# Nystrom attention and a top-1 expert layer on one core: q and k of three batches turned on TensorE, the pseudo-inverse on eight tiles and in pairs, output in blocks of 32 rows, a refitted planner

## Chip, cores, metric

One of the cores of a Trainium2 chip runs one program. The metric is the device time of one execution in microseconds; lower is better. Input and output lie in device memory.

## What is computed

Eight batches of eight heads, 576 positions, head size 64. Nystrom attention with 32 landmarks (each the mean of 18 neighbouring positions), then an expert layer over the 4608 rows, in which each row goes to the expert with the greatest logit.

```python
q_lm = q.reshape(B, H, m, S // m, D).mean(axis=3)      # m = 32; k_lm the same from k
A, Bm, C = sm(q, k_lm), sm(q_lm, k_lm), sm(q_lm, k)    # softmax of scaled products
Z = Bm.T / (norm1(Bm) * norminf(Bm) + 1e-06)
for _ in range(6):
    Z = 2 * Z - Z @ Bm @ Z
x = (A @ Z @ C @ v)                                    # -> (4608, 512)
e = argmax(x @ w_gate)
out = softmax(x @ w_gate)[e] * sigmoid(x @ w_output_gate)[e] * (relu(x @ w1[e]) @ w2[e])
```

Attention is in f32, the expert layer in bf16. The kernel takes for each batch its most frequent expert as the main one. Rows of other experts are done by a loop at the end that reads a count of them and is skipped when it is zero.

## The kernel before

**Attention of a batch** (`batch`, from line 388) goes in two halves of four heads, 32 partitions a head and landmark. SyncE brings k, q and v (lines 403 and 406) into three buffers each. VectorE turns k and q in blocks of 32 x 32 (line 415). The landmark sums are five additions, which the planner gives to GpSimd or VectorE (434 to 438), and a turn of the sums (442). TensorE makes the scores of k and q against the landmarks from 32 x 32 tiles, two passes over the head size (459, 461). The scores of k go through a maximum (466), an exponential on ScalarE (470, 471), six turns on TensorE (480), an evacuation (482) and the product with v (491). Those of q are turned, normalised over the landmarks and turned back on VectorE, GpSimd and ScalarE (508 to 529).

**The pseudo-inverse** (533 to 611) of a batch: the scores of landmarks (542), a softmax, column sums, and seven iterations. An iteration is 16 small matmuls (587: X'X and X'Y of four heads, first one half and then the other, on the same four 32 x 32 tiles of the array) and a step on VectorE, 2X minus the product in PSUM (597, 602, 605). Batch 0 takes its halves as steps of their own.

**Routing** (613 to 731): the result is turned, multiplied by the gates and by the attention weights (627, 639); VectorE finds the expert of each row and the batch's main one in some twenty small instructions (656 to 709). Then x is formed (720) and written as bf16.

**The expert layer** (733 to 787): GpSimd reads the main expert and brings its w1 and w2 in halves, with a cast to bf16, by eight DMAs (335, 338, 342), into one of two buffers (even and odd batches); a load whose expert is already in the buffer is skipped. For the up product 8 x 2 blocks of four matmuls of 128 x 288 (759) are evacuated with a relu on ScalarE (365). For the down product five tiles of rows, four of 128 and one of 64, are eight matmuls of 512 columns each (774), scaled (781 or 783) into one of four y buffers and written out by one DMA a tile (786), whose access pattern is 4 (or 2) positions x 32 landmarks x 512.

**The order of the work** isn't written out. Each operation is given to `Plan` (72 to 234) with its engines and costs in ns, its reads and writes, a priority (`PR` by batch for attention, `FR` for the expert layer, lines 269 and 270) and a mode (the tile shape on TensorE). `run` plays a list schedule with these costs, chooses engine and buffer for each, and emits the instructions in the order of their planned starts. On the chip each engine then takes its instructions strictly in that order. `CAPA` and `CAPF` limit the PSUM banks in use by attention and by the expert layer.

Of the kernel before, what the change touches and what calls it, by code (L numbers as in the profile page):

```python
# [22 lines left out]
F32 = mybir.dt.float32  # L23
# [43 lines left out]
class Op:  # L67
    __slots__ = ("engs", "fn", "deps", "new", "vals", "prio", "lag", "end", "eng", "nd", "succ", "load", "seq",
# [3 lines left out]
class Plan:  # L72
# [3 lines left out]
    LAT = 90.0  # L76
    PE_LAG = 150.0
# [4 lines left out]
    FETCH = 3800.0  # L82

# [5 lines left out]
    def op(self, engs, fn, r=(), w=(), hold=(), prio=0.0, lag=0.0, load=0.0, mode=None, after=(), bias=0.0, shy=(), recs=0):  # L89
# [8 lines left out]
        o.deps = set(after)  # L98
        o.new = []
# [19 lines left out]
        for v in o.vals:  # L119
            if v in o.new:  # L120
                v.first = o
            if v.tag is not None:
                o.deps.add(v.first)
            v.users.add(o)
        o.deps.discard(o)
        self.ops.append(o)
        return o

    def run(self):
        free = {}  # L130
        for o in self.ops:
            o.nd = len(o.deps)
            o.succ = []
        for o in self.ops:
            for d in o.deps:
                d.succ.append(o)
# [6 lines left out]
        dma = 0.0  # L143
# [4 lines left out]
        while ready:  # L148
            cands = []
            for o in ready:  # L150
# [19 lines left out]
                for e, c in o.engs.items():  # L170
                    st = max(free.get(e, 0.0), slot_t)
                    for d in o.deps:
                        st = max(st, d.end + (self.LAT if d.eng != e else 0.0))
                    if e == "PE" and o.mode != mode:
                        st = max(st, free.get(e, 0.0) + self.SWITCH)
                    cands.append((st, st + c, o, e))
# [5 lines left out]
            for st, en, o, e in cands:  # L182
                if o not in best_per or en + o.shy.get(e, 0.0) < best_per[o][1] + o.shy.get(best_per[o][2], 0.0):
# [5 lines left out]
                    key=lambda p: (p.prio, p.seq))  # L189
            st, en, e = best_per[o]  # L190
# [15 lines left out]
            free[e] = en  # L206
            busy[e] = busy.get(e, 0.0) + en - st
            if o.load:
                dma = max(dma, en) + o.load
                o.end = dma + o.lag  # L210
            else:
                o.end = en + o.lag + (self.PE_LAG if e == "PE" else 0.0)
# [25 lines left out]
def kernel(  # L238
# [28 lines left out]
    SHY = 1100.0  # L267
    SHYE = 400.0
    PR = [0.0, 1.0, 2.0, 3.0, 4.0, 5.0, 6.0, 7.0]
    FR = [3.5, 4.5, 5.5, 5.25, 7.5, 8.5, 9.5, 10.5]  # L270
    PESUM = 0
    SPLIT = (0,)
    CAPA = 2
    CAPF = 2
    LASTF = 5
    LOAD = 2050.0
    WLOAD = 5000.0
# [14 lines left out]
    e8 = pool.tile([128, E], F32, name="e8")  # L292
    e0 = pool.tile([128, E], F32, name="e0")
    pad = pool.tile([128, E], F32, name="pad")
    wgs = pool.tile([128, HH, 2 * E], F32, name="wgs")
# [14 lines left out]
    t_lm = tag("lm", 4, [128, 2, 2, m])  # L310
    t_EC = tag("EC", 1, [128, 2, U2])
    t_ECT = tag("ECT", 1, [PT, 6, 128])
    t_At = tag("At", 2, [128, g, m])
    t_AT = tag("AT", 4, [128, UP])
    t_XW = tag("XW", 2, [128, 2, m + D])
    t_X = tag("X", 4, [128, 2, m + D])
    t_sm = tag("sm", 8, [128, 64])
    t_co = tag("co", B, [128, NT])
    t_ZT = tag("ZT", 2, [128, 128])
    t_G = tag("G", 2, [128, 2, m])  # L320
    t_lg = tag("lg", 2, [128, NT, m])
    t_rt = tag("rt", 2, [128, 8, NT, E])
# [9 lines left out]
    def ask_w1(dst, e, part, **new):  # L332
        f_ = slice(part * F // 2, (part + 1) * F // 2)
        w = moe_w1[bass.ds(e, 1)]
        nc.gpsimd.dma_start(out=dst[:, :2, f_], in_=w.rearrange("e (c p) f -> p (e c) f", p=128)[:, :2, f_], **new)  # L335
        src = w.rearrange("e (c a p) f -> a p (e c) f", a=2, p=D)
        for a in range(2):
            nc.gpsimd.dma_start(out=dst[a * D:(a + 1) * D, 2:, f_], in_=src[1 - a, :, 2:, f_], **new)

    def ask_w2(dst, e, part, **new):  # L340
        c_ = slice(part * FCH // 2, (part + 1) * FCH // 2)
        nc.gpsimd.dma_start(out=dst[:, c_], in_=moe_w2[bass.ds(e, 1)].rearrange("e (c p) d -> p (e c) d", p=128)[:, c_], **new)

    with tc.manual_schedule():
# [5 lines left out]
        nc.vector.tensor_copy(e0, ei)  # L350
        ri = pool.tile([128, B, NT], I32, name="ri")
        for h in range(HH):
            nc.gpsimd.iota(ri[h * m:(h + 1) * m], pattern=[[S, B], [HH, NT]], base=h, channel_multiplier=g)
        nc.vector.tensor_copy(rows, ri)
        nc.vector.tensor_scalar(out=e8, in0=e0, scalar1=8.0, scalar2=None, op0=ADD)
        for t in t_AT.tiles:
            nc.gpsimd.memset(t[:, S:], 0.0)
        for t in t_G.tiles:
            nc.gpsimd.memset(t, 0.0)

# [15 lines left out]
        def evac(n):  # L376
            return {"ACT": 140 + 0.95 * n, "DVE": 90 + 1.1 * n}
# [4 lines left out]
        def bring_gates(e):  # L382
            for hf in range(2):
                for i, w in enumerate((moe_w_gate, moe_w_output_gate)):
                    nc.sync.dma_start(out=wgs[hf * D:(hf + 1) * D, :, i * E:(i + 1) * E],
                                      in_=w[hf * HH * D:(hf + 1) * HH * D].rearrange("(h d) e -> d h e", d=D))

        def batch(b):
            pr = PR[b]
            lms, ATs, sms, ZVp = [], [], [], []  # L390
            XW = Val(t_XW)
            P.op({"": 0}, lambda e: None, w=[XW["home"]], prio=pr)
            for hf in range(2):
# [14 lines left out]
                if b == 0 and hf == 1:  # L408
                    P.op({"SP": 2500}, bring_gates, w=[gates[0]], prio=pr, lag=2500)
                    P.op({"POOL": 400}, lambda e: nc.gpsimd.tensor_scalar(  # L410
                        out=wgs[:, :, E:], in0=wgs[:, :, E:], scalar1=-1.0, scalar2=None, op0=MUL),
                        w=[gates[0]], prio=pr + .5)
                Ts = {"q": Val(t_T["q"]), "k": Val(t_T["k"])}
                for x in "kq":
                    P.op({"DVE": 1370}, lambda e, T=Ts[x], n=ns[x], x=x: nc.vector.transpose(  # L415
                        out=T.t.rearrange("p j (t r) -> p t j r", r=m) if x == "q" else
                        T.t.rearrange("p j (t w r) -> p w t j r", t=6, w=3),
                        in_=n.t.rearrange("p t (j c) -> p t j c", j=2) if x == "q" else
                        n.t.rearrange("p (w t) (j c) -> p w t j c", j=2, w=3)),
                        r=[ns[x][0]], w=[Ts[x][0]], prio=pr + .01)  # L420
                s9 = Val(t_s9) if b >= PESUM else Val(p_M, "attn", CAPA)
                for i, x in ((1, "k"), (0, "q")):
                    if b < PESUM:
                        def sums_pe(e, n=ns[x], s9=s9, i=i):
                            for t in range(g):
                                nc.tensor.matmul(s9.t[:, i * D:(i + 1) * D], lhsT=I128, rhs=n.t[:, t, :],
                                                 start=(t == 0), stop=(t == g - 1))
                        P.op({"PE": 2050}, sums_pe, recs=72, r=[ns[x][0]], w=[s9[i]], mode=(128, 128), prio=pr + .005)
                        continue
                    s3 = Val(t_s3)  # L430

                    def sums(e, n=ns[x], s9=s9, s3=s3, i=i):
                        eng = nc.gpsimd if e == "POOL" else nc.vector
                        eng.tensor_tensor(s3.t, n.t[:, :9], n.t[:, 9:], op=ADD)  # L434
                        eng.tensor_tensor(s3.t[:, :4], s3.t[:, :4], s3.t[:, 4:8], op=ADD)
                        eng.tensor_tensor(s3.t[:, :2], s3.t[:, :2], s3.t[:, 2:4], op=ADD)
                        eng.tensor_tensor(s3.t[:, 0], s3.t[:, 0], s3.t[:, 1], op=ADD)
                        eng.tensor_tensor(s9.t[:, i], s3.t[:, 0], s3.t[:, 8], op=ADD)
                    P.op({"POOL": 3200, "DVE": 1750}, sums, r=[ns[x][0]], w=[s9[i], s3[0]], prio=pr + .005, shy={"DVE": SHY})
                lm = Val(t_lm)  # L440
                lms.append(lm)
                P.op({"DVE": 270}, lambda e, lm=lm, s9=s9: nc.vector.transpose(  # L442
                    out=lm.t.rearrange("p x j r -> p (x j r)"),
                    in_=s9.t[:, :128] if b < PESUM else s9.t.rearrange("p x d -> p (x d)")),
                    r=[s9[0], s9[1]], w=[lm[0]], prio=pr + .02)
# [5 lines left out]
                sms.append(st)  # L451

                def scores(e, pC=pC, pA=pA, lm=lm, Ts=Ts):
                    for n in range(2):
                        for j in range(2):
                            for h in range(HH):
                                r_ = slice(h * m, (h + 1) * m)
                                o = (h + 2) % HH
                                nc.tensor.matmul(pC.t[o * m:(o + 1) * m, n, :U2], lhsT=lm.t[r_, 0, j, :],  # L459
                                                 rhs=Ts["k"].t[r_, j, n * U2:(n + 1) * U2], start=(j == 0), stop=(j == 1))  # L460
                                nc.tensor.matmul(pA.t[r_, n, :U2], lhsT=lm.t[r_, 1, j, :],  # L461
                                                 rhs=Ts["q"].t[r_, j, n * U2:(n + 1) * U2], start=(j == 0), stop=(j == 1))
                P.op({"PE": 1950}, scores, recs=128, r=[lm[0], Ts["k"][0], Ts["q"][0]], w=[pC[0], pA[0]], hold=[EC, At, st],
                     mode=(32, 32), prio=pr + .03)

                P.op({"DVE": 760}, lambda e, pC=pC, st=st: nc.vector.tensor_reduce(  # L466
# [6 lines left out]
                P.op({"ACT": 1150}, c_exp, r=[pC[0], st[0]], w=[EC[0], st[1]], prio=pr + .03)  # L473
# [3 lines left out]
                def ec_turn(e, pE=pE, EC=EC):  # L477
                    f = EC.t.rearrange("p a c -> p (a c)").rearrange("p (t c) -> p t c", t=6)
                    for c in range(6):
                        nc.tensor.transpose(pE.t[:PT, c // 3, (c % 3) * 128:(c % 3 + 1) * 128], in_=f[:, c], identity=I128)  # L480
# [391 lines left out]
```

## Time and profile before

| what | value |
|---|---|
| three runs | 336.76, 338.63, 343.56 us; median 338.63 |
| the profiled execution | 341.74 us, span 340.1 us |
| TensorE | busy 265.4 us, 78% of the span, mean granted clock 0.913 |
| VectorE | busy 199.5 us, 59% |
| ScalarE, GpSimd | busy 146.3 and 137.7 us |
| DMA | 49.02 MB in 28294 packets, mean 144 GB/s |

A row of a group reads: line, engine, operation, output<-input with shapes, count | busy us in all, mean ns of one | idle us of the engine just before them, and what ended it. A row of the timeline reads: start us, length us, engine, line, operation, count. Lines are those of the kernel before. Durations of matmuls overlap, since they are pipelined.

### The profile page before, as it was taken

The numbers are of one execution on the slowest core, as the hardware profiler recorded it, in microseconds if no ns is written. First come the engines' busy times: TensorE is split into PE (matmuls) and PEld (weight loads), VectorE is DVE, ScalarE is ACT, GpSimd is POOL, SyncE is SP. The second block draws the span as 40 slices with busy tenths as digits, with TensorE's granted clock in tenths as the row PEclk, the third lists the DMA queues.
The fourth block names the chain that finished last, engine by engine and source line by source line (L and its number), as shares of the span: only waits on it lengthen the run. The fifth ranks groups of instructions, "written<-read, shape, count | busy, mean of one in ns | idle before, by whom it ended". The sixth has DMA issues, their size and how long they took to land. (4 is left out here: it accounts for less than half of the span.)

```text
span 340.1 us, 10916 instructions
## 1 busy us (share of the span) xinstructions
PE 265.4 (78%) x4525; PEld 169.9 (50%) x4537; DVE 199.5 (59%) x542; ACT 146.3 (43%) x356; POOL 137.7 (40%) x225
## 2 busy tenths in 40 slices
PE   0466755896998799599899997399999975996950
PEld 0134543464745477457557755276667433654520
DVE  4698978797897896689816936459441430500000
ACT  1033233245535555156465743157365332743420
POOL 3659899569766973752001213232020060150000
PEclk9956969699999799899999999789999995999795
DMA  7999747559958977476212315817021159196221
GB/s 279 255 328 255 212 143 202 125 139 206 191 162 235 201 237 189 108 220 232 94 53 77 83 39 160 139 17 114 2 64 63 40 123 209 33 168 130 91 84 62
DMA packets 28294, 49.02 MB, mean 144 GB/s; under 512 B 3152, under 2 KB 19536, under 8 KB 28240
## 3 DMA queue, kind: packets, MB, share of 16 engines
q1 hardware_dynamic: 17360, 37.79, 35.9%
q0 software_dynamic: 10880, 10.49, 20.1%
q8 instruction: 37, 0.61, 0.7%
q14 instruction: 17, 0.14, 0.1%
HBM read 61.90 MB, written 9.44 MB: 210 GB/s over the span
## 5 line engine op out<-in xcount | busy, mean ns | idle before, releaser
L759 PE MATMUL M<-xT_all,w 128*128 128x288 bf16 x512 | 75.2, 298 | 19.3 <-DMA w<-in_moe_w_dram 11.9
L774 PE MATMUL M<-w,hT 128*128 128x512 bf16 (+1 forms) x309 | 73.6, 381 | 0.6
L759 PEld LDWEIGHTS <-w 128*128 128x128 bf16 x512 | 50.3, 102 | 38.5 <-issue 12.6
L365 ACT ACTIVATE hT<-M 128x288 bf16<-128x288 f32 x128 | 50.4, 410 | 31.6 <-PE M L759 27.4
L459 PE MATMUL S<-Tk,lm 32*32 32x288 f32 x512 | 43.6, 467 | 11.4 <-DVE lm L442 11.4
L774 PEld LDWEIGHTS <-hT 128*128 128x128 bf16 (+1 forms) x320 | 30.8, 101 | 33.5 <-issue 1.1
L461 PE MATMUL S<-Tq,lm 32*32 32x288 f32 x512 | 41.1, 465 | 0.0
L781 ACT ACTIVATE y<-M,co 128x512 f32<-128x512 f32 (+1 forms) x38 | 25.8, 685 | 34.1 <-PE M L774 24.7
L335 POOL DMA_DIRECT2D w<-in_moe_w_dram x16 | 7.8, 489 | 74.1 <-DVE X L602 35.4
L459 PEld LDWEIGHTS S<-Tk,lm 32*32 32x32 f32 x512 | 25.2, 119 | 18.3 <-DVE lm L442 11.1
L587 PE MATMUL M<-X 32*32 32x96 f32 x768 | 26.8, 252 | 9.2 <-DVE X L602 6.8
L516 POOL TENSOR_TENSOR At<-At,sm 128x576 f32<-128x576 f32 x16 | 18.6, 1161 | 30.6 <-DVE sm L511 23.4
L602 DVE SCALAR_TENSOR_TENSOR X<-X,M 128x192 f32<-128x192 f32 (+1 forms) x45 | 13.9, 315 | 27.6 <-PE M L587 27.6
L587 PEld LDWEIGHTS M<-X 32*32 32x32 f32 x768 | 17.4, 107 | 23.1 <-DVE X L602 8.4
L525 POOL TENSOR_TENSOR At<-At,sm 128x576 f32<-128x576 f32 x16 | 18.7, 1166 | 24.9 <-DVE sm L523 15.8
L470 ACT ACTIVATE sm<-sm 128x1 f32<-128x1 f32 x16 | 3.2, 203 | 51.7 <-DVE sm L466 51.7
L367 ACT CAST xT_all<-S 128x576 bf16<-128x576 f32 x31 | 18.6, 640 | 13.7 <-PE S L720 13.7
L434 POOL TENSOR_TENSOR s<-nk 128x576 f32<-128x576 f32 x13 | 18.3, 1407 | 14.9 <-DMA nk<-in_k_dram 8.0
L529 DVE STREAM_TRANSPOSE AT<-At 128x576 f32<-128x576 f32 x16 | 12.3, 769 | 17.7 <-POOL At L525 10.3
L480 PE MATMUL S<-I,EC 128*96 128x128 f32 x96 | 16.1, 313 | 7.9 <-ACT EC L471 5.4
L415 DVE STREAM_TRANSPOSE Tk<-nk 128x1152 f32<-128x1152 f32 x16 | 21.7, 1358 | 0.1
L415 DVE STREAM_TRANSPOSE Tq<-nq 128x1152 f32<-128x1152 f32 x16 | 21.5, 1346 | 0.0
(111 smaller groups left out, 406.2 us busy)
## 6 DMA issues: line engine op xcount, KB each, us to landing
nk<-in_k_dram SPq DMA_DIRECT2D x16, 576.0 KB
nq<-in_q_dram SPq DMA_DIRECT2D x16, 576.0 KB
nv<-in_v_dram SPq DMA_DIRECT2D x48, 192.0 KB
w<-in_moe_w_dram POOLq DMA_DIRECT2D x16, 512.0 KB
out_dram<-y SPq DMA_DIRECT2D x32, 256.0 KB
w<-in_moe_w_dram POOLq DMA_DIRECT2D x16, 256.0 KB
w<-in_moe_w_dram POOLq DMA_DIRECT2D x32, 128.0 KB
out_dram<-y SPq DMA_DIRECT2D x8, 128.0 KB
```

The source lines that it names most:

```text
L365: nc.scalar.activation(out=dst(), in_=src(), func=RELU)
L367: nc.scalar.copy(dst(), src())
L415: P.op({"DVE": 1370}, lambda e, T=Ts[x], n=ns[x], x=x: nc.vector.transpose(out=T.t.rearrange("p j (t r) -> p t j r", r=m) if x == "q" else ...
L434: eng.tensor_tensor(s3.t, n.t[:, :9], n.t[:, 9:], op=ADD)
L459: nc.tensor.matmul(pC.t[o * m:(o + 1) * m, n, :U2], lhsT=lm.t[r_, 0, j, :], rhs=Ts["k"].t[r_, j, n * U2:(n + 1) * U2], start=(j == 0), sto ...
L461: nc.tensor.matmul(pA.t[r_, n, :U2], lhsT=lm.t[r_, 1, j, :], rhs=Ts["q"].t[r_, j, n * U2:(n + 1) * U2], start=(j == 0), stop=(j == 1))
L516: P.op({"POOL": 1160}, lambda e, At=At, st=st: nc.gpsimd.tensor_tensor(At.t, At.t, b_l(st.t[:, 8:8 + g]), op=SUB), r=[st["ax"]], w=[At[0]] ...
L525: P.op({"POOL": 1160}, lambda e, At=At, st=st: nc.gpsimd.tensor_tensor(At.t, At.t, b_l(st.t[:, 32:32 + g]), op=MUL), r=[st["as"]], w=[At[0 ...
L587: nc.tensor.matmul(pN.t[r_, hf * W:(hf + 1) * W], lhsT=cur.t[r_, hf, :m], rhs=cur.t[r_, hf, :])
L759: nc.tensor.matmul(ph.t[:, :NH], lhsT=w1.t[:, dc, fc * 128:(fc + 1) * 128], rhs=xT.t[:, dc, n * NH:(n + 1) * NH], start=(dc == 0), stop=(d ...
L774: nc.tensor.matmul(py.t[:tk, :], lhsT=hTs[fc].t[:, i * 128:i * 128 + tk], rhs=w2.t[:, fc, :], start=(fc == 0), stop=(fc == FCH - 1))
L781: nc.scalar.activation(out=y.t[:tk], in_=py.t[:tk, :], func=COPY, scale=com.t[:tk, i:i + 1])
```

## The change

1. **q and k of batches 0 to 2** (`PET = 3`) are turned on TensorE: 18 turns of 128 x 128 a half into PSUM, and evacuations of 512 and 128 columns by ScalarE or VectorE. The sums are turned by four matmuls. The scores of these batches then contract over 64 rows in one pass, 16 matmuls a half instead of 32.
2. **The pseudo-inverse** keeps its two halves on eight tiles of the array (half 1 shifted by two column groups, in a second bank) and accumulates in PSUM; factors of two and the sign are in the scaling. A step is a plain scaled copy, in three pieces, on ScalarE or VectorE. Batches 4 and 5, and 6 and 7, are solved together.
3. **Output**: a DMA writes 32 rows (SP: four a tile; the last two tiles of the last batch go half from SP and half from ScalarE's queue). The tile of 64 rows is made as two halves of 256 columns on two column groups, and scaled as one 128 x 256 tile.
4. **Smaller ones**: position order by even and odd; w1 in two DMAs of 64 partitions, and in whole loads for batches 2 to 5 (`WHALF`); the gates as one 128-row product; fewer small routing instructions; a row sum on VectorE in one instruction; a relu may go to VectorE; the count of strays formed once at the end.
5. **The planner**: new costs, latencies and priorities, three banks each for attention and expert layer, a rule that lets an engine wait for a more urgent operation.

```diff
-    LAT = 90.0
-    PE_LAG = 150.0
+    LAT = 50.0
+    SAME = 34.0
+    LAG = 95.0
+    PE_LAG = 185.0
+    DRAIN = {(32, 64): 178.0, (128, 32): 140.0, (64, 32): 125.0, (32, 32): 125.0, (128, 64): 130.0}
...
+            better = [p for p in best_per if best_per[p][2] == e and p.prio < o.prio - self.MARGIN
+                      and best_per[p][0] < best_per[o][1]]
...
-    FR = [3.5, 4.5, 5.5, 5.25, 7.5, 8.5, 9.5, 10.5]
-    CAPA = 2
-    CAPF = 2
+    PR = [-0.2, 0.8, 1.9, 3, 4, 4.8, 6.0, 6.9]
+    FR = [3.25, 3.25, 5.5, 7.25, 7.5, 7.75, 8.5, 8.5]
+    PET = 3
+    WHALF = (0, 1, 6, 7)
+    GROUPS = ((0,), (1,), (2,), (3,), (4, 5), (6, 7))
+    CAPA = 3
+    CAPF = 3
...
+                            def turn(e, pT=pT, ns=ns, what=what):
+                                for c, (y, t) in enumerate(what):
+                                    nc.tensor.transpose(pT.t[:, c * 128:(c + 1) * 128],
+                                                        in_=ns[y].t[:, 2 * t:2 * t + 2].rearrange("p t d -> p (t d)"), identity=I128)
...
+                        if e == "DVE":
+                            nc.vector.tensor_reduce(s9.t[:, i], n.t.rearrange("p t d -> p d t"), axis=X, op=ADD)
+                            return
...
+                    if wide:
+                        for x, p in (("k", pC), ("q", pA)):
                             for h in range(HH):
+                                for n in range(2):
+                                    one(n, x, h, 0, (h + 2) % HH if x == "k" else h, p, True)
...
+                                o = (h + 2 * hf) % HH
+                                nc.tensor.matmul(pN[hf].t[o * m:(o + 1) * m, i * W + lo:(i + 1) * W],
+                                                 lhsT=cur.t[r_, u, :m] if it else nx.t[r_, u], rhs=cur.t[r_, u, lo:],
+                                                 start=(it == 0 and i == 0), stop=True, skip_group_check=True)
...
+                        if e == "ACT":
+                            nc.scalar.mul(o, i_, c)
+                        else:
+                            nc.vector.tensor_scalar(out=o, in0=i_, scalar1=c, scalar2=None, op0=MUL)
...
+                            for a in range(2):
+                                nc.tensor.matmul(py.t[a * D:(a + 1) * D, :HD // 2], lhsT=hTs[fc].t[:, i * 128:S],
+                                                 rhs=w2.t[:, fc, a * HD // 2:(a + 1) * HD // 2], **f)
...
+                by = ("SP", "ACT") if b == B - 1 and i >= NT - 2 else ("SP",)
...
+                        to = out[b * S:(b + 1) * S].rearrange("(r t n) d -> n t r d", t=g // 2, n=2)
+                        for j in range(tk // m):
+                            u = HH * i + j
+                            for a in range(HD // n):
+                                if (j + a) % len(by) == part:
+                                    (nc.scalar if e == "ACT" else nc.sync).dma_start(
+                                        out=to[u // (g // 2), u % (g // 2), :, a * n:(a + 1) * n],
+                                        in_=y.t[(a * 2 + j) * m:(a * 2 + j + 1) * m, :n])
```

In the new order of instructions TensorE's first expert matmul stands behind all 108 turns, five of the six halves' scores of batches 0 to 2, the whole inverse of batch 0 and four of seven iterations of batch 1's. Before, it stood behind six halves' scores and both inverses. The last instructions on TensorE are, as before, the up and down products of the last batches, now those of 5, 6 and 7.

More of the change, by code (lines that the diff above doesn't have):

```diff
@@ L376, in evac @@
         def evac(n):
-            return {"ACT": 140 + 0.95 * n, "DVE": 90 + 1.1 * n}
+            return {"ACT": 78 + 0.81 * n, "DVE": 55 + 1.035 * n}
         xTs, coms = {}, {}
@@ L421, in batch @@
-                s9 = Val(t_s9) if b >= PESUM else Val(p_M, "attn", CAPA)
-                for i, x in ((1, "k"), (0, "q")):
[L423 to L429, printed above, removed]
+                wide = b < PET
@@ L467, in batch @@
+                P.op({"PE": 980 if wide else 1950}, scores, recs=64 if wide else 128,
+                     r=[lm[0]] + [Ts[x][u] for x in "kq" for u in range(3)], w=[pC[0], pA[0]], hold=[EC, At, st],
+                     mode=(D, m) if wide else (m, m), prio=pr + .03)
+                P.op({"DVE": 660}, lambda e, pC=pC, st=st: nc.vector.tensor_reduce(
                     st.t[:, 0:1], pC.t[:, :, :U2], axis=XY, op=MAX), r=[pC[0]], w=[st[0]], prio=pr + .03)
@@ L528, in batch, with solve @@
                 ATs.append(AT)
-                P.op({"DVE": 800}, lambda e, At=At, AT=AT: nc.vector.transpose(
+                P.op({"DVE": 685}, lambda e, At=At, AT=AT: nc.vector.transpose(
                     out=AT.t[:, :S], in_=At.t.rearrange("p k r -> p (k r)")),
                     r=[At[0]], w=[AT[0]], prio=pr + .035)
-            pr = PR[b] + 0.1
+        def solve(bs, XW):
+            pr = PR[bs[-1]] + 0.1
+            nb = len(bs)
+            U = 2 * nb
+            wide = [b < PET for b in bs]
+            units = [(hf * nb + i, hf, i) for hf in range(2) for i in range(nb)]
+            xk, yk = [XW[f"x{u}"] for u in range(U)], [XW[f"y{u}"] for u in range(U)]
+            lms = [lms_of[bs[i]][hf] for _, hf, i in units]
@@ new lines, in solve, with b_nx @@
+            P.op({"DVE": 435 + 65 * U}, b_cc, r=[pS[0]], w=[sb[3], nx[0]], prio=pr + .025)
+            def b_nx(e):
+                if e == "ACT":
+                    for u in range(U):
+                        nc.scalar.mul(nx.t[:, u], XW.t[:, u, :m], sb.t[:, 20 + u:21 + u])
+                else:
+                    nc.vector.tensor_tensor(nx.t[:, :U], XW.t[:, :U, :m], b_l2(sb.t[:, 20:20 + U]), op=MUL)
+            P.op({"ACT": 215 * U, "DVE": 500 + 70 * U}, b_nx, r=[sb[3]] + xk, w=[nx[0]], prio=pr + .025)
@@ L585, in pinv @@
+            pN = [Val(p_M, "attn", CAPA) for _ in range(2)]
+            W = m + D
+            parts = [(0, slice(0, 128), slice(0, 128)), (1, slice(0, D), slice(D, 128)), (1, slice(D, 128), slice(0, D))]
+            cur, ck = XW, xk + yk
+            for it in range(7):
+                def pinv(e, cur=cur, it=it):
+                    lo = 0 if it < 6 else m
+                    for i in range(nb):
+                        for hf in range(2):
+                            u = hf * nb + i
                             for h in range(HH):
@@ L729, in batch, with cuts, ask1 @@
             reg = {}
-            def ask1(e, part):
-                if part == 0:
+            halves = 2 if b in WHALF else 1
+            def cuts(n):
+                return [slice(i * n // halves, (i + 1) * n // halves) for i in range(halves)]
+            def ask1(e, f_):
+                if f_.start == 0:
                     reg["e"] = nc.values_load(
```

501 lines of the change are left out of this document (286 added, 215 removed).

## The prediction

> **What bounds the kernel now.** I read the page's first two parts first, for where TensorE works and where it doesn't.
>
> ```profile
> span 340.1 us, 10916 instructions
> PE 265.4 (78%) x4525; PEld 169.9 (50%) x4537; DVE 199.5 (59%) x542; ACT 146.3 (43%) x356; POOL 137.7 (40%) x225
> PE   0466755896998799599899997399999975996950
> PEclk9956969699999799899999999789999995999795
> DVE  4698978797897896689816936459441430500000
> DMA  7999747559958977476212315817021159196221
> ```
>
> TensorE is idle for 340.1 - 265.4 = 74.7 us, most of it in the first nine slices and the last two. In those nine VectorE is the full engine. So I cut the span where the first expert matmul starts (74.3 us) and where TensorE ends, and asked for the engines' busy time by stretch.
>
> ```profile
> 74.33 1.16 PE L759 MATMUL M<-xT_all,w 128*128 128x288 bf16 x8
> ...
> 0.00:74.30 74.30, 42.85 (x1073) 28.02 (x1074) 59.29 (x137) 19.56 (x48) 52.35 (x89) 0.82 0.75 214
> 74.30:140.00 65.70, 55.05 (x1072) 36.66 (x1069) 52.51 (x137) 33.45 (x89) 47.22 (x72) 0.97 0.84 203
> 140.00:200.00 60.00, 58.23 (x876) 38.49 (x879) 44.64 (x112) 33.36 (x79) 14.88 (x28) 0.97 0.36 112
> 200.00:260.00 60.00, 51.02 (x1014) 34.79 (x1015) 32.13 (x104) 29.41 (x73) 12.60 (x22) 0.94 0.38 84
> 260.00:327.60 67.60, 58.22 (x500) 31.99 (x501) 10.95 (x55) 29.80 (x67) 10.68 (x16) 0.92 0.52 104
> 327.60:340.10 12.50, 0.00 (x0) 0.00 (x0) 0.00 (x0) 0.68 (x1) 0.00 (x0) 0.69 0.20 77
> ```
>
> Columns: stretch, length, then busy us (and count) of PE, PEld, DVE, ACT, POOL, granted clock, DMA share, GB/s. Three parts show. In the front (74.3 us) DVE is busy 59.29, PE 42.85, ACT 19.56. In the middle (253.3 us) PE is busy 222.5, about 88%: PE is the bound, and its 31 us of idle time are single waits. In the tail (12.5 us) only a DMA moves. The middle's waits on PE, from the list of who waited for whom, and ScalarE's in the front:
>
> ```profile
> PE M L759 <- DMA w<-in_moe_w_dram: 11.9, 4, 4.4
> PE M L759 <- DVE X L602: 4.3, 2, 3.4
> PE M L759 <- ACT y L781: 2.9, 1, 2.9
> ACT sm L470 <- DVE sm L466: 51.7, 12, 16.2
> ```
>
> **The front: 74.3 to about 62 us, -12.** These rows carry it: the transposes and row sums that feed the scores, and TensorE's own turns at two clocks.
>
> ```profile
> L415 DVE STREAM_TRANSPOSE Tk<-nk 128x1152 f32<-128x1152 f32 x16 | 21.7, 1358 | 0.1
> L415 DVE STREAM_TRANSPOSE Tq<-nq 128x1152 f32<-128x1152 f32 x16 | 21.5, 1346 | 0.0
> L442 DVE STREAM_TRANSPOSE lm<-s 128x128 f32<-128x128 f32 x16 | 4.6, 290 | 0.1
> L602 DVE SCALAR_TENSOR_TENSOR X<-X,M 128x192 f32<-128x192 f32 (+1 forms) x45 | 13.9, 315 | 27.6 <-PE M L587 27.6
> L367 ACT CAST xT_all<-S 128x576 bf16<-128x576 f32 x31 | 18.6, 640 | 13.7 <-PE S L720 13.7
> L373 DVE CAST xT_all<-S 128x576 bf16<-128x576 f32 x1 | 0.7, 747 | 0.0
> L373 DVE COPY ZT<-M 128x128 f32<-128x128 f32 x2 | 0.5, 272 | 0.0
> L459 PE MATMUL S<-Tk,lm 32*32 32x288 f32 x512 | 43.6, 467 | 11.4 <-DVE lm L442 11.4
> 5.31 0.76 DVE L434 TENSOR_TENSOR s<-nk 128x576 f32<-128x576 f32 x1 [2.08 <-DMA nk<-in_k_dram]
> 19.50 1.49 PE L480 MATMUL S<-I,EC 128*96 128x128 f32 x6 [4.21 <-ACT EC L471]
> 38.93 0.86 PE L480 MATMUL S<-I,EC 128*96 128x128 f32 x6 [0.24 <-ACT EC L471]
> ```
>
> DVE loses twelve transposes of q and k (12 x 1.35 = 16.2 us), six of the sums (1.7), and about fifteen of the pseudo-inverse's steps that the new order gives to ACT (5). It gains three evacuations of 512 columns, four of 128 and two of 256: by the rows of 576 and 128 columns 3 x 0.7 + 4 x 0.27 + 2 x 0.4 = 4 us. The new order also puts the scores of batch 2's second half behind the first expert matmul (some 4 us less on DVE). 59.3 - 16.2 - 1.7 - 5 + 4 - 4 = 36; the front's other DVE edits (one long row sum where there were five short ones) I leave within plus 4. ACT takes 21 of the 512-column evacuations (0.6 each), a dozen small ones and 30 steps of 0.2 to 0.3: 19.6 + 23 = 43 us. PE gets 108 turns and 24 matmuls that turn the sums, at (0.86 - 0.15)/6 = 0.12 us each: 16 us; scores of five halves at half of 43.6/16 = 2.7 us where there were six at 2.7: -9.5; fewer steps of the inverse: -3; one half's later work: -2. So 42.9 + 1.5 = 44 us. No engine then needs over 45 of the 57 us between the first landing (5.3) and 62.
> Bounds: if DVE kept its present pace (59.29 in 69.0, 86%) and were still the bound, 40/0.86 + 5.3 = 52; the DMAs forbid much less, since 0.75 x 74.3 = 56 us of all engines' time were moved there, some 50 of them needed. Upward: if the turns keep the clock at half, a turn takes 1.49/6 = 0.25 us, and 44 us at clock 0.82 become 44 x 0.82/0.5 = 72, the front 77. I take 62, nearer the lower end because the chains on ACT and DVE can't be packed wholly.
> The Trainium skill, TensorE: Matmul & The Clock Gate, Part 4, says that a transpose on TensorE doesn't count as activity, so that full speed "doesn't engage". The trace has six turns in a row at both speeds (1.49 and 0.86 us) but no long train of them, so no run here shows it; by the rule the sum ends as in the second rival below.
>
> **Less work for PE behind the front: -13, and +2.**
>
> ```profile
> L587 PE MATMUL M<-X 32*32 32x96 f32 x768 | 26.8, 252 | 9.2 <-DVE X L602 6.8 <-ACT y L781 1.0 <-DVE sm L547 0.7
> 159.64 0.53 PE L587 MATMUL M<-X 32*32 32x96 f32 x16
> 299.79 3.62 PE L774 MATMUL M<-w,hT 128*128 128x512 bf16 x16
> 307.63 1.91 PE L774 MATMUL M<-w,hT 128*64 128x512 bf16 x8
> ```
>
> An iteration of the inverse runs its two halves one after the other on the same four tiles (0.53 us with its 0.24 us of drain). On eight tiles both go at once: (0.53 - 0.24)/2 = 0.15 us saved, in 6 batches x 7 iterations = 6.3 us. That eight tiles run at once is what the scores show: 512 records of 467 ns in 43.6 us is 5.5 at a time from one of its two lines alone. Bounds: 0, if the second tile row waits, and half of the 0.53: 11.
> The last 64 rows of a batch cost 1.91 us for 8 matmuls, as much as 128 rows (3.62 for 16). As two halves of 256 columns on two column groups they would take half: 8 batches x 8 x 0.105 = 6.7 us. Bounds: 0 (one after the other) and 6.7.
> The half that was put behind the front costs PE some 2 us there. The gate and logit edits (16 matmuls fewer a batch at a few tens of ns) I leave at nothing, under 1 us. Pairs halve the number of chains for batches 4 to 7; what that spares in drains is within the next term. All evacuations and steps that ACT gains there lie beside PE: ACT is busy 29 to 33 us of each 60; without that cover it would be 0.2 to 0.3 us a step. A batch whose solve waits for its partner comes later; the new order fills that time with downs and ups of the batches before, four to eight matmuls between iterations.
>
> **Waits in the middle: -9.** The y wait (2.9) goes with the output's queue, below. Of the 11.9 us on weights I take half: whole loads for batches 2 to 5 halve the number of DMAs on POOL, but the front, shorter by 12 us, makes every later due time tighter. 2.9 + 6 = 9. Bounds: 0 and 2.9 + 11.9 = 15.
>
> **The tail: -6.**
>
> ```profile
> L786 SPq DMA_DIRECT2D out_dram<-y x40: 529/537/3564, 98.5 to 329.4; - x40
> 328.74 0.68 ACT L781 ACTIVATE y<-M,co 64x512 f32<-64x512 f32 x1 [2.29 <-PEq L807]
> 329.45 0.54 SPq L786 DMA_DIRECT2D out_dram<-y  x1
> 0.88 0.41 SPq L406 DMA_DIRECT2D nk<-in_k_dram  x1
> 13.07 2.09 SPq L403 DMA_DIRECT2D nv<-in_v_dram  x3
> 331.00:332.00 1.00, 0.00 (x0) 0.00 (x0) 0.00 (x0) 0.00 (x0) 0.00 (x0) 1.00 0.26 102
> 336.00:338.00 2.00, 0.00 (x0) 0.00 (x0) 0.00 (x0) 0.00 (x0) 0.00 (x0) 0.50 0.13 51
> 338.00:340.10 2.10, 0.00 (x0) 0.00 (x0) 0.00 (x0) 0.00 (x0) 0.00 (x0) 0.50 0.02 9
> ```
>
> After the last issue (329.99) the outputs still drain to about 338, at 0.26 of sixteen DMA engines, then 0.13: four engines for a tile of 4 x 32 rows, two for the last of 2 x 32. A DMA of 32 rows has 32 as its slowest dimension on both sides and can go over all sixteen; the queue then empties as fast as it is filled. The price is issues: 160 instead of 40, at 0.537 us, 64 us more on SP. A tile then needs 2.1 us of SP, where PE makes one in 3.62/2 = 1.8 us. In the last batch SP, with two tiles shared with ACT, issues 16 x 0.537 = 8.6 us against PE's 8, and starts one tile late: about 2 us of SP behind the last y. So 2, and 2 for landing (an estimate: two engines at 51 GB/s need 2.6 us for the last 128 KB), and 2 for the end, where there were 329.42 to 340.1 = 10.7: -5, and 1 more because the 64-row tile is made and scaled in half the time: -6. Bounds: 0, if the many small issues cost what the wide ones did, and -8.5.
> The Trainium skill, DMA: Bandwidth & Descriptors, section on why a DMA increments its semaphore by 16, says that a copy takes the largest number of engines up to 16 that divides both sides' slowest dimensions; the shares 0.26 and 0.13 agree (four and two of sixteen).
>
> **The sum** is made against the profiled execution, 341.7 us (span 340.1 and 1.6 around it), which is 3.1 above the median of 338.6: 341.7 - 12 - 13 + 2 - 9 - 6 = 303.7, so 304.
>
> **Rivals.** (1) The clock stays low under the turns: front 77, +3 instead of -12, the rest as above: 341.7 + 3 - 13 + 2 - 9 - 6 = 319. For it: clock 0.82 in the front already, and 1.49 us turns. Against it: lower-speed stretches follow idle ones, and the turns fill idle time.
> (2) Loads become the front's bound and weights stay late: front 68, waits unchanged: 341.7 - 6 - 13 + 2 - 0 - 6 = 319. For it: a DMA share of 0.75 in a front that is to shrink; against it: behind its fourth slice the front's DMA share falls to 0.4 to 0.7 in four slices of five.
> (3) The change doesn't do what it says: column halves and tiles run one after the other, the front stays at 74, and only the tail is gained: 341.7 + 2 - 6 = 338, no change. Against it: the scores' overlap.
> (4) Slower: SP. Every input of a later batch is queued there behind outputs that wait for y. At 0.537 us the 160 issues take 86, and 84 of inputs 32 x 0.41 + 52 x 0.7 = 49. The longest issue shown took 3.564 us, when earlier ones had not been taken; if the mean came to 1.9 us, 160 x 1.9 + 49 = 353 us, and SP would set the end there; from 1.85 us on it decides. The median of 537 speaks against it.
>
> **Numbers.** Forecast 0.50, (1) 0.17, (2) 0.17, (3) 0.08, (4) 0.08. The forecast's own range: terms at -22, -18, +2, -15, -8.5 give 280, which needs every bound at once, and at -5, -6, +2, 0, 0 give 333; halfway to each from 304, 290 to 318. With (1) and (2) inside and a margin for the runs' spread (336.8 to 343.6, about 1%), the range is 286 to 326. About 2% is what a measurement of this kernel can tell from no change. Forecast, (1) and (2) are faster by more: 0.84. (3) is the same, 0.08. (4) is slower, 0.08.
>
> **What will show it.** Right: first expert matmul near 62 us; turns near 0.12 us each and a front clock above 0.8; 64-row downs at about 1 us for a batch's sixteen; an iteration of one batch under 0.45 us; DMA share near 0.5 or more while outputs leave, and 6 us behind the last y. Wrong: a first expert matmul after 70; PE waiting for the weights' DMA by over 12 us; SP's outputs issued over 3 us behind their y; PE's idle time filled with waits for ACT's steps.

## The result, and the profile after

The changed kernel takes 281.1 us (median of 4 runs, 279.7 to 284.5), the kernel before 339.0 beside it: ratio 0.830, interval 0.822 to 0.838. It is faster by 58 us. That is below the predicted range, whose low end was 286. The profiled execution of the kernel before was one of its slower ones (341.7 us against a median of 338.6), so the spans below differ by 62 us.

The page of the changed kernel, first two parts, and the stretches cut at the same events as before (first expert matmul, end of TensorE's last). The columns are those of the prediction's second fence.

```profile
span 278.1 us, 10846 instructions
PE 250.8 (90%) x4452; PEld 159.9 (58%) x4453; DVE 177.7 (64%) x420; ACT 179.1 (64%) x497; POOL 129.7 (47%) x204
PE   3878778789999799999969999999999999999990
PEclk9999999999999999999998999999999999999997
DVE  5978667998888889989695799777625610100001
DMA  7999999799899868545994453595300599995143
```

```profile
0.00:59.39 59.39, 44.28 (x885) 30.81 (x887) 45.49 (x95) 38.67 (x114) 39.57 (x75) 1.00 0.97 248
59.39:270.80 211.41, 206.49 (x3569) 129.12 (x3567) 131.07 (x321) 140.47 (x385) 90.12 (x129) 0.99 0.70 159
...
270.80:278.10 7.30, 0.00 (x1) 0.00 (x0) 1.13 (x5) 0.00 (x0) 0.00 (x0) 0.78 0.34 79
```

| stretch | before | after | change | predicted |
|---|---|---|---|---|
| front | 74.3 | 59.4 | -14.9 | -12 |
| middle, TensorE busy | 222.5 | 206.5 | -16.0 | -11 |
| middle, TensorE idle | 30.8 | 4.9 | -25.9 | -9 |
| tail | 12.5 | 7.3 | -5.2 | -6 |
| span | 340.1 | 278.1 | -62.0 | -38 |

The front and the tail came out near their terms, and TensorE's work 5 us beyond its own. The idle time of the middle, 31 us of single waits, went almost wholly where a third of it had been forecast to go: that is 17 of the 24 us between forecast and profile. So two theories were set against each other. Order: the waits went because the planner now lays the instructions out as the chip runs them. Structure: they went because the work is lighter and the loads and outputs leave sooner.

### The profile page after: what moved, and what is told of

Read it like the earlier page. It is cut to its first block, busy times and chain, and to the rows that moved or that the text cites. A ratio compares the mean times of both kernels' runs of the same rounds, so it can differ in the third digit from the quotient of the medians.

```text
span 278.1 us, 10846 instructions
## 1 busy us (share of the span) xinstructions
PE 250.8 (90%) x4452; PEld 159.9 (58%) x4453; DVE 177.7 (64%) x420; ACT 179.1 (64%) x497; POOL 129.7 (47%) x204
## 4 chain that ended last, share of the span: by engine, by line
PE 76%; DVE 8%; ACT 5%; issue 4%; DMA 3%; POOL 2%; SPq 0%; DVEq 0%; POOLq 0%; ACTq 0%
PE M L882 22%; PE M L899 21%; PE S L534 9%; PE M L708 5%; PE S L837 4%; PE M L576 4%; PE S L564 3%; DMA nq<-in_q_dram 3%; PE M L902 3%; PE M L755 2%; ACT X L722 1%; PE M L467 1%; ACT EC L556 1%; PE M L638 1%; DVE At L595 1%
## 5 line engine op out<-in xcount | busy, mean ns | idle before, releaser
L882 PE MATMUL M<-xT_all,w 128*128 128x288 bf16 x512 | 71.4, 287 | 4.2 <-issue 3.3
L899 PE MATMUL M<-w,hT 128*128 128x512 bf16 x256 | 62.0, 386 | 0.0
L899 PEld LDWEIGHTS <-hT 128*128 128x128 bf16 x256 | 24.0, 100 | 27.5 <-issue 3.7
L722 ACT ACTIVATE X<-M 64x96 f32<-64x96 f32 (+3 forms) x92 | 24.9, 271 | 14.2 <-PE M L708 10.9
L603 POOL TENSOR_TENSOR At<-At,sm 128x576 f32<-128x576 f32 x16 | 18.6, 1165 | 30.6 <-DVE sm L598 29.5
L911 ACT ACTIVATE y<-M,co 128x512 f32<-128x512 f32 (+1 forms) x29 | 19.2, 672 | 16.7 <-PE M L899 12.2
L534 PE MATMUL S<-Tq,lm 32*32 32x288 f32 (+1 forms) x416 | 26.8, 404 | 2.1 <-issue 2.0
L612 POOL TENSOR_TENSOR At<-At,sm 128x576 f32<-128x576 f32 x16 | 18.5, 1156 | 19.0 <-DVE sm L610 6.0
L534 PE MATMUL S<-Tk,lm 32*32 32x288 f32 (+1 forms) x416 | 26.0, 406 | 0.8 <-ACT ECT L402 0.6
L495 POOL TENSOR_TENSOR s<-nq 128x576 f32<-128x576 f32 x12 | 16.9, 1408 | 5.5 <-DMA nq<-in_q_dram 5.5
L708 PE MATMUL M<-X 32*32 32x96 f32 (+1 forms) x768 | 18.4, 245 | 0.5 <-ACT X L722 0.5
L576 PE MATMUL M<-nv,ECT 96*32 96x64 f32 x768 | 14.8, 221 | 3.1 <-issue 1.9
L496 POOL TENSOR_TENSOR s<-s 128x256 f32<-128x256 f32 x22 | 16.0, 727 | 1.7
L708 PEld LDWEIGHTS M<-X 32*32 32x32 f32 x768 | 10.8, 103 | 10.4 <-ACT X L722 5.7
L534 PEld LDWEIGHTS S<-Tq,lm 32*32 32x32 f32 (+1 forms) x416 | 12.9, 105 | 6.1 <-issue 2.8
```

The source lines that it names most:

```text
L495: nc.gpsimd.tensor_tensor(s3.t, n.t[:, :9], n.t[:, 9:], op=ADD)
L534: nc.tensor.matmul(p.t[o * m:(o + 1) * m, n, :U2], lhsT=l_of(lm, wide, 0 if x == "k" else 1, h, n if wide else j), rhs=t_of(Ts[x], x, wide ...
L576: nc.tensor.matmul(pV.t[h * m:(h + 1) * m, :D], lhsT=ECT.t[:, c, o * m:(o + 1) * m], rhs=n.t[:, h, c * D:(c + 1) * D], start=(c == 0), sto ...
L603: P.op({"POOL": 1115}, lambda e, At=At, st=st: nc.gpsimd.tensor_tensor(At.t, At.t, b_l(st.t[:, 8:8 + g]), op=SUB), r=[st["ax"]], w=[At[0]] ...
L612: P.op({"POOL": 1115}, lambda e, At=At, st=st: nc.gpsimd.tensor_tensor(At.t, At.t, b_l(st.t[:, 32:32 + g]), op=MUL), r=[st["as"]], w=[At[0 ...
L708: nc.tensor.matmul(pN[hf].t[o * m:(o + 1) * m, i * W + lo:(i + 1) * W], lhsT=cur.t[r_, u, :m] if it else nx.t[r_, u], rhs=cur.t[r_, u, lo: ...
```

## The experiments

Each kernel was timed beside the kernel before, and its ratio is to that. The changed kernel's ratio is 0.830; differences against it are differences of such ratios times 339 us. By the intervals, a difference under some 4 us is not clear of the spread of the runs. The stretches (front, middle, tail) are those of one profiled execution each.

**The old planner under the new work.** `class Plan` of the kernel before; op costs, priorities and bank limits as changed.

> The changed kernel with the planner class of the kernel before (its latencies, its list rule); the work, the op costs, the priorities and the bank limits stay the changed ones. Order theory (TensorE's waits behind the front, 30.8 us before and 4.9 after, went because the planner now orders the instructions as the chip runs them): they come back in good part, +15 to +30 us over 281, so 296 to 311. Structure theory (they went because the work itself is lighter and the loads and outputs leave sooner): at most +6, under 288.

309.2 us, ratio 0.907 (0.897 to 0.917): +26. The stretches of this kernel (front, middle):

```profile
0.00:71.63 71.63, 52.30 (x991) 36.21 (x992) 51.21 (x100) 45.13 (x134) 42.00 (x77) 0.88 0.89 227
71.63:301.67 230.04, 212.36 (x3470) 132.50 (x3462) 124.61 (x311) 139.01 (x367) 81.45 (x117) 0.96 0.63 139
```

The front is 12.2 us longer, TensorE's idle time in the middle is 230.0 - 212.4 = 17.7 instead of 4.9, and its busy time there is 5.9 longer. The total is the order theory's, but it put all of it on the waits behind the front: of the 25.9 us of idle time that had gone, 12.8, about half, came back, and the front, which the theory didn't name, makes up as much.

**The new planner under the old work**, with the new costs, priorities and bank limits.

> The kernel before with the new planner class, the new op costs where the op is the same, the new priorities and three banks each; all work as before. Order theory: the waits behind the front fall by half or more, 310 to 325 us (front and tail hardly moved, nothing of TensorE's work saved). Structure theory: 333 to 342, no change.

329.8 us, ratio 0.970 (0.957 to 0.982), 10 us less: between both. The front fell to 64.5 us and TensorE's idle time in the middle to 251.3 - 235.4 = 15.9, the half that the order theory asked for, but 6.1 us of the latter were waits for y (2.9 before). TensorE's busy time for the same work rose from 265.4 to 273.4 us, which used up most of the rest; why isn't shown.

**Turns, pairs, tiles, halves**: four undone one at a time.

```diff
-    PET = 3
+    PET = 0
```

> The changed kernel with no batch turned on TensorE (PET = 0; all q and k turned on VectorE, replanned). Both theories: the first expert matmul moves from 59 back to 70 to 74 us, TensorE's work falls by 10, and the time rises by the front alone, 291 to 296. Under the structure theory VectorE, with 16 us more to do, also delays the middle: 298 or more, with waits for VectorE on TensorE.

295.5 us, ratio 0.868 (0.858 to 0.878): +13. First expert matmul at 70.0, VectorE busy 56.8 us before it (45.5 with the turns), the granted clock 0.81 there (1.00 in the changed kernel's profile, 0.88 to 1.00 in all runs here with the turns). Middle +4. The time and the front are as both theories expected, TensorE's work isn't: its busy time fell by 2 us in all (250.8 to 248.9), not by 10, since the scores in two passes take 45.0 us of it instead of 30.6, against the 16.4 of the turns.

```diff
-    GROUPS = ((0,), (1,), (2,), (3,), (4, 5), (6, 7))
+    GROUPS = tuple((b,) for b in range(8))
```

> The changed kernel with every batch solved by itself (replanned). Order theory: 281 to 285, since single chains can be filled as well. Structure theory: four chains of seven iterations where two were, each with a 1.2 us period that the expert matmuls must fill: 287 to 292, with waits of TensorE for the inverse's steps.

290.4 us, ratio 0.853 (0.844 to 0.863): +8. The middle is 219.1 us: TensorE is busy 211.5 (+5.0) and idle 7.6 (+2.7). The pairs spare TensorE busy time that I had costed at nothing, not only waits: the iterations' matmuls (L708), as many in both kernels, are busy for 26.1 us without pairs and 21.8 with them.

```diff
-            parts = [(0, slice(0, 128), slice(0, 128)), (1, slice(0, D), slice(D, 128)), (1, slice(D, 128), slice(0, D))]
+            parts = [(0, slice(0, 128), slice(0, 128)), (1, slice(0, D), slice(0, D)), (1, slice(D, 128), slice(D, 128))]
...
-                                o = (h + 2 * hf) % HH
+                                o = h
```

> The changed kernel with both halves of the inverse on the same four tiles of the array (half 1 no longer shifted by two column groups; nothing else, the planned costs too). If eight tiles run at once as I took it: an iteration of one batch 0.15 us longer, of a pair 0.30, 42 + 14 chances on batches in all 8 x 7 x 0.15 = 8 us of TensorE work, 286 to 289. If the steps' chain and not TensorE sets the pace there: 281 to 283.

287.6 us, ratio 0.846 (0.838 to 0.853): +5. An iteration of one batch on eight tiles (first row, the changed kernel) and on four (second):

```profile
83.08 0.39 PE L708 MATMUL M<-XW,nx 32*32 32x96 f32 x16
```

```profile
85.82 0.53 PE L708 MATMUL M<-XW,nx 32*32 32x96 f32 x16
```

0.14 us an iteration, where 0.15 was forecast.

```diff
-                            if tk == 128:
-                                nc.tensor.matmul(py.t, lhsT=hTs[fc].t[:, i * 128:(i + 1) * 128], rhs=w2.t[:, fc, :], **f)
-                                continue
-                            for a in range(2):
-                                nc.tensor.matmul(py.t[a * D:(a + 1) * D, :HD // 2], lhsT=hTs[fc].t[:, i * 128:S],
-                                                 rhs=w2.t[:, fc, a * HD // 2:(a + 1) * HD // 2], **f)
+                            nc.tensor.matmul(py.t[:tk], lhsT=hTs[fc].t[:, i * 128:i * 128 + tk], rhs=w2.t[:, fc, :], **f)
...
```

The scaling, the output and the planned costs of this tile go with it.

> The changed kernel with the 64-row tile as 64 rows by 512 columns again (one matmul instead of two halves; scaled and written as 64 rows). 8 x 0.85 = 6.8 us of TensorE work more, all of it where TensorE is the bound: 287 to 289. If the halves' gain is hidden: 281 to 283.

285.3 us, ratio 0.839 (0.832 to 0.847): +3, between both expectations and not clear of the spread, though TensorE's busy time in the middle rose by the forecast 6.8 (213.3). Idle 5.9 (+1.0); front and tail came out 0.6 and 1.9 shorter, and the rest lies within the runs' spread.

**The output's form.** First undone in the changed kernel, with all outputs from SP. Tile 2 crosses the even and odd half there, so some DMAs have 3 positions or 1.

```diff
-                        for j in range(tk // m):
-                            u = HH * i + j
...
+                                    out=to[nn, t0:t0 + len(js), :, a * n:(a + 1) * n],
+                                    in_=y.t[(a * 2 + js[0]) * m:(a * 2 + js[-1] + 1) * m, :n])
```

> The changed kernel with the widest output DMAs that the position order allows (4, 3, 2 or 1 positions x 32 rows in one, seven a batch instead of twenty, all from SP; the planned costs unchanged). If the few engines of such a DMA were the cost: DMA share 0.13 to 0.27 while outputs leave, the time behind TensorE's last matmul back from 7.3 to 11 or 12 us, and some waits for y buffers: 285 to 290. If the issues on SP are now the cost: 277 to 280.

307.0 us, ratio 0.906 (0.898 to 0.914): +26, three to six times what was expected. Its middle, and who waits for the output and for y (us in total, times, longest us):

```profile
58.37:290.23 231.86, 210.42 (x3551) 132.65 (x3567) 129.98 (x321) 140.02 (x384) 90.18 (x129) 0.95 0.61 144
```

```profile
DVE y L913 <- DMA out_dram<-y: 32.4, 3, 17.2
ACT y L911 <- DMA out_dram<-y: 15.8, 3, 7.6
PE M L882 <- ACT y L911: 7.2, 1, 7.2
PE M L902 <- ACT y L911: 4.2, 1, 4.2
PE M L882 <- DVE y L913: 3.0, 2, 2.3
```

The front is unchanged (58.4). The middle is 20 us longer, 16.5 of it TensorE's idle time: y buffers stay full, ScalarE and VectorE stand 48 us waiting for one, and TensorE behind them for 14.4. The tail is 13.2. SP alone for the last two tiles has little part in that: `one_queue` below costs 1 us. How long the last two 512 KB loads of weights take to land (last column, median us), there and then in the changed kernel:

```profile
w<-in_moe_w_dram POOLq DMA_DIRECT2D x2, 512.0 KB, 15.4
```

```profile
w<-in_moe_w_dram POOLq DMA_DIRECT2D x2, 512.0 KB, 9.2
```

These two are issued while only outputs and weights move. In the seven other kernels with the new list rule and 32-row outputs whose trace has this landing, they take 7.9 to 9.2 us. The pair near 176 us, beside which no output leaves, takes 6.9 in both kernels; the pair near 76 us, beside inputs and the first outputs, 13.5 in the changed kernel and 15.5 here. The form isn't the only thing that delays them: with the old list rule, where six or more other loads stand just before the last pair, it takes 15 us beside 32-row outputs too.

Then done alone in the kernel before, with its own order of instructions:

```diff
-                P.op({"SP": 550}, lambda e, i=i, tk=tk, y=y: nc.sync.dma_start(
-                    out=out[b * S:(b + 1) * S].rearrange("(r t) d -> t r d", t=g)[HH * i:HH * i + tk // m], in_=y.t[:tk]), r=[y[0]], prio=fr, lag=2000, load=900)
+                def leave(e, i=i, tk=tk, y=y):
+                    to = out[b * S:(b + 1) * S].rearrange("(r t) d -> t r d", t=g)
+                    for j in range(tk // m):
+                        nc.sync.dma_start(out=to[HH * i + j], in_=y.t[j * m:(j + 1) * m])
```

> The kernel before, in its own order of instructions, with 32 rows in each output DMA (four or two a tile, all from SP; the planned cost unchanged). The narrow DMAs' cost there as its trace shows it: 2.9 us of TensorE waiting for y and some 5 behind the last y, so 339 goes to 330 to 334. If the added issues hold up the inputs on SP: 338 or more.

319.1 us, ratio 0.934 (0.923 to 0.946): -22, well beyond the 330 to 334 expected, and twice what replanning alone gave in this kernel. Its stretches and waits:

```profile
0.00:73.45 73.45, 44.71 (x1074) 28.59 (x1075) 58.78 (x137) 19.59 (x48) 52.54 (x89) 0.86 0.76 216
73.45:311.10 237.65, 219.15 (x3466) 139.24 (x3463) 140.97 (x406) 126.57 (x307) 85.50 (x137) 0.98 0.61 136
...
311.10:318.90 7.80, 0.00 (x1) 0.00 (x0) 0.00 (x0) 0.68 (x1) 0.00 (x0) 0.67 0.36 93
```

```profile
PE M L759 <- DMA w<-in_moe_w_dram: 5.3, 4, 2.7
PE M L759 <- DVE X L602: 0.9, 1, 0.9
```

The tail gives 4.7, as forecast. The middle gives 15.6: TensorE idle 18.5 instead of 30.8. The 2.9 us for y are gone, but the waits for weights also fell from 11.9 to 5.3, with no edit to the weights' loads. The packets of GpSimd's queue, which carries the weights, show part of the reason (packets, MB, share of 16 engines): first the kernel before and then this one, in the first 14.5 us of the same load of 2.10 MB, that of the second to last batch; last the kernel before from 289.2 to 296.0, the end of that load.

```profile
q0 software_dynamic: 2033, 1.96, 85.1%
q0 software_dynamic: 2175, 2.10, 93.4%
...
q0 software_dynamic: 222, 0.22, 19.2%
```

With the 32-row output the load is through in 14.5 us. In the kernel before it takes 19.4, and its last 0.22 MB go for 6.8 us over a fifth of the engines' time.

> The replanned kernel before (329.8) with 32 rows in each output DMA, its order unchanged. If the output's drain became the limit as soon as the order let TensorE run faster: its 6 us of waits for y, as much again on ScalarE, and 5 behind the last y go, 312 to 319, more than the same edit gives in the old order. If the gains merely add: 322 to 325.

316.4 us, ratio 0.933 (0.924 to 0.941). The time lies in the first range, but not by its reason: the output takes 13 us off the replanned kernel, less than the 22 it takes off the old order, and the replanning takes nothing measurable off the kernel with the new output. The gains overlap. Idle time in the middle is 245.0 - 234.2 = 10.8.

**Inside the planner.** Without the block that begins with `better =`, and with `LAT = 90`, `SAME = LAG = 0`, `PE_LAG = 150`, `DRAIN = {}`, `SHARE = 0`:

> The changed kernel whose planner lacks only the rule that lets an engine wait for, or first fill the time before, a more urgent operation; all numbers stay. If the rule carries what the old planner lost (28 us): 295 to 305. If the numbers carry it: 281 to 287.

325.2 us, ratio 0.954 (0.940 to 0.967): +42, beyond the range and more than the whole old planner. Idle 253.9 - 217.7 = 36 in the middle.

> The changed kernel whose planner keeps the new rules but counts with the old latencies (90 between engines, none on the same engine, 150 behind TensorE, 95 for any change of tile shape, POOL's loads not slowed by SP's). If the latencies carry what the old planner lost: 295 to 305. If the rule does: 281 to 287.

291.6 us, ratio 0.862 (0.853 to 0.871): +11. Below the 295 to 305, above the 281 to 287. Both matter, the rule most. The first is worse than the old planner, which has neither; that rule and numbers are fitted to each other would explain it, but isn't shown.

> The changed work under the old planner class with the old priorities too (op costs, bank limits, pairs stay). If the 28 us of the old planner were only a mismatch between it and the new priorities: 285 to 298. If the old list rule cannot order the new work: 305 to 320.

311.4 us, ratio 0.914 (0.907 to 0.921), as with the new priorities (0.907): no mismatch with those.

**Loads, queue, a fourth batch.** `WHALF` for all batches; `by = ("SP",)`; `PET = 4`.

> The changed kernel with all weights in halves (batches 2 to 5 too). I had taken the whole loads as the reason for half of the spared waits for weights. If so, TensorE waits for weights again and the time is 284 to 290. If the output's form and the order spared them: 279 to 283.

289.9 us, ratio 0.853 (0.847 to 0.860): +8, but TensorE has no wait for weights in it. It is idle 11.1 in the middle, 3.4 of it for the exponential of the scores. So the range was met and its reason wasn't: whole loads did not spare the waits for weights. What made the new order worse isn't shown.

> The changed kernel with the last two tiles written from SP alone. SP's issues at 0.42 us (the changed kernel's median) need 20 x 0.42 = 8.4 us for the last batch, so some 1 to 2 us more behind TensorE's last matmul: 282 to 283.5. If the landing and not the issue ends the kernel: 281.

282.0 us, ratio 0.832 (0.828 to 0.836): tail 8.2 instead of 7.3, as expected, and not told apart in the runs.

> The changed kernel with a fourth batch turned on TensorE (PET = 4). It gives TensorE 2 x 1.4 us more and spares VectorE 5.4 us in the stretch from 60 to 110 us, where TensorE is busy 95% and VectorE 86%: 282 to 287 if TensorE is the bound there, as its idle time says; under 280 if VectorE still is.

287.1 us, ratio 0.842 (0.835 to 0.849): +4, at the edge of the spread. In the profile the front is 4.7 us longer (64.1) and the middle 2.5, so that the loss isn't shown to be TensorE's as the bound behind the front. A fourth batch doesn't help. No variant beat the changed kernel.

## Why the prediction was right and where it failed

**The front, -12: right in its number (-14.9), in part by its mechanism.** Without the turns it is 70, but with them under the old planner it is 71.6: it needs both, and the working didn't name the planner. The old work replanned, with no turns, has a front of 64.5, since its order puts more behind the first expert matmul (747 matmul records stand before it there, 1073 in the kernel before, 885 in the changed one). TensorE's 44 us of busy time there came out at 44.3 (46.6 in `one_queue`, whose front is the same), VectorE's 36 to 40 at 45.5. That the number fits is partly luck.

**The cold clock (rival 1): wrong.** The rows of the changed kernel's first turns:

```profile
4.86 1.94 PE L467 MATMUL M<-I,nk 128*128 128x128 f32 x8 [4.86 <-DMA nk<-in_k_dram]
6.59 1.91 PE L467 MATMUL M<-I,nq 128*128 128x128 f32 x8
...
8.66 0.60 PE L467 MATMUL M<-I,nk 128*128 128x128 f32 x4
9.68 0.66 PE L509 MATMUL M<-I,s 128*64 128x128 f32 x8 [0.42 <-DVE s L493]
...
11.99 1.09 PE L467 MATMUL M<-I,nq 128*128 128x128 f32 x8
```

Eight turns take 1.9 us at first and 1.09 later, and the step comes before 8.7, when TensorE had run nothing but turns for 3.8 us. The column of the granted clock doesn't show this step: it stands at 1.00 on both sides. So here turns, in f32, do bring full speed, against the rule of the Trainium skill (TensorE: Matmul & The Clock Gate, Part 4); the measurement decides. The prediction's sentence on that rule points to the second rival and means the first.

**TensorE's work, -13 and +2: right in both rows it priced** (0.14 us an iteration for 0.15; 16 halves in 1.06 us where 8 wide ones took 1.91), wrong in costing the pairs at nothing: they spare 5 us of busy time, as much as the middle's work beat its term by. That isn't the whole account, since the 512 up products, the same in both kernels, took 71.4 us instead of 75.2, with a granted clock of 0.99 in the middle instead of 0.95; nothing priced that.

**Waits in the middle, -9: the step that failed.** They fell by 25.9. "The y wait (2.9) goes with the output's queue" took the 2.9 us that TensorE was seen to wait as the price of narrow output DMAs in the middle. The kernel before with nothing but the 32-row output shows 12.3 us less idle time. A load of weights goes over all engines (the DMA share is at its full 1 while most of the load above runs, 276.6 to 289.2 us), and the engines that also carry an output are late with their part: that fits its end on a fifth of the engines' time, and the last two loads of `wide_out`, 15.4 us where the changed kernel's took 9.2. That the waits for VectorE's step (4.3 to 0.9) shrank by the same way is only argued. The second half of the term, whole weight loads, was not the cause. The other cause is the planner, costed at nothing. TensorE's idle time in the middle, in us:

| | old order or planner | new planner |
|---|---|---|
| old work, wide output | 30.8 | 15.9 |
| old work, 32-row output | 18.5 | 10.8 |
| new work, 32-row output | 17.7 | 4.9 |
| new work, wide output | not run | 21.4 |

So the 32-row output is worth 5 to 17 us of it and the planner 8 to 15, each by what else is there, and the new work takes away up to 6 or, under wide output, adds as much. The order and the output's drain hold TensorE up in the same places, and no single split of the 25.9 is right.

**The tail, -6: right** (-5.2). SP took 0.42 us an issue, less than the 0.537 assumed, and rival 4 had no ground. Rival 2's condition came in part: the front's DMA share rose from 0.75 to 0.97, but the front is 59 us and not 68, and TensorE waits for no weights. Whether the loads now set the front's length wasn't tried. Rival 3's didn't come: the halves and tiles overlapped.

**The range** ended at 286 since 280 "needs every bound at once". It didn't need that: front and tail stayed well within their bounds, TensorE's work came to its own (-16), and the waits alone passed theirs, -25.9 where the bound was -15, because that counted only the y and weight waits, 14.8 of the 31 us. (Halfway from 304 to 280 is 292, not the 290 of the working.)

The undone parts sum to more than the whole (26 + 13 + 8 + 5 + 3 + 26 = 81 against 58), so none is the gain of its part by itself. Planner and output overlap the other way in the kernel before: 10 and 22 us alone, 23 together. What the pairs, the tiles or the turns give alone in the kernel before wasn't tried.

## What to carry to other kernels

Look at how many DMA engines each transfer uses before looking at its bytes: where the share is a quarter while outputs leave, other loads can pay too, and a wait for weights can be the output's. When an engine is 88% busy and its idle time lies in many single waits of different kinds, the order of instructions is a term of its own, to be bounded by the whole idle time. Don't add the losses of parts undone in a plan that was made for them all, and read the waits of a run, not its time alone: two of these runs met their ranges for another reason than the one expected.

## What was not expected of the hardware

A train of f32 turns alone raised TensorE's speed after about 3.5 us in the changed kernel (0.24 to 0.12 us a turn), with the granted clock at 1.00 throughout. Beside output DMAs of up to four positions the last two 512 KB weight loads landed in 15.4 us, and in 7.9 to 9.2 beside outputs of 32 rows. An output DMA of 32 rows took SP 0.42 us (median of 156), less than the 0.54 (median of 40) of one with 128 or 64.
